# Retention attention followed by two FFN layers on one core: chunk 6 and a decay table loaded behind more weight halves, and VectorE's work of an early step in another order

## The chip, the cores and the metric

The kernel runs on one core of one Trainium2 chip. The metric is the device time of one execution in microseconds. Five engines run side by side, each through its own list of instructions in order: TensorE (PE; its weight loads are shown as PEld), VectorE (DVE), ScalarE (ACT), GpSimd (POOL) and SyncE (SP), which here only issues transfers.

## What is computed

The reference first runs a linear attention with decay ("retention") over 768 positions for 2 batches and 8 heads of 64, and then two feed-forward layers of width 512 to 2048 to 512, the first with Mish, the second with ELU:

```python
for t in range(S):
    state = gamma * state + einsum('bhd,bhe->bhde', k[:, :, t], v[:, :, t])
    y[:, :, t] = scale * einsum('bhd,bhde->bhe', q[:, :, t], state)
x = y.transpose(0, 2, 1, 3).reshape(1536, 512)
h = x @ w_in                      # layer 0
x = (h * tanh(softplus(h))) @ w_out
h = x @ w_in2                     # layer 1
out = where(h > 0, h, exp(min(h, 0)) - 1) @ w_out2
```

## The kernel before

**Retention in chunks.** The positions are cut into 12 chunks of 128 (6 for each batch, taken in turn, numbered 0 to 11). A chunk c has two loads of 512 KB, `qk` and `kv`. GpSimd multiplies its q by a decay table into `qd` (`scale_q`, L202; four of the tables, `tab`, are loaded by `load_tab`) and its k by another into `kd` (`scale_k`, L187). From chunk 4 on, TensorE does a chunk in two parts. `scores64` makes the score products (L304) and the state products (L311, from `kd`); its second half, the function `rest` that it returns, is VectorE's: two mask multiplies into `at` (L319) and one or two state sums (L326). `attend64` then multiplies states by `qd` (L348) and v by `at` (L355); its `rest` is a copy of one part on ScalarE (`t`, L367), two sums on VectorE (`y`, L370), the rounded high part on ScalarE (`xh`, L372) and the low part on VectorE (`xl`, L374). There is one buffer each for `at`, `kd` and `qd`, three for `qk` and `kv`.

**The feed-forward layers.** Every fp32 product is made of three passes with operands split into a high part and a low part. A "tile" n is one 128-wide slice of a layer's 2048 hidden columns against 512 positions. `up(n)` is 12 matmuls (L396): 4 with high weights `w0h`, 4 with low weights `w0l`, 4 with the low part of x. `mish(n)` evaluates Mish twice on ScalarE (`gh`, then `h` itself, L416 and L417) and takes the low part `gl` as their difference on VectorE (L418). `down(n - 3)` is 12 matmuls (L453), three tiles later.

**Weights.** They come as 64-bit words and are unpacked on the chip, in 64 halves k of 512 KB through four staging buffers `st`. For a half: `fetch` issues the load (L109); `dec_fields` extracts fields on ScalarE (L116, L118); `dec_join` puts the bits together on VectorE (L127 for all its halves, then L133), and issues the next `fetch`, which waits for that L133, because it reuses the buffer; `dec_split` rounds to `w0h` or `w1h` on ScalarE (L146) and takes `w0l` or `w1l` as the difference on GpSimd (L147). Half 3 is the first half of weight chunk 3, which `up(3)` reads.

**The order** is written out by hand. After a prologue (chunks 0 to 3 and the first three halves) a loop runs over n = 0, 1, 2, ...; `steps` says which chunk parts belong to a step:

```python
steps = {0: [(scores64, 4, ta)], 3: [(attend64, 6), (scores64, 7)], 4: [(attend64, 7)]}
for n in (1, 2):
    steps[n] = [(attend64, n + 3, tb), (scores64, n + 4, ta)]
```

In a step come: `up(n)` and the matmuls of the chunk parts, `mish(n)`, the `rest` functions with `scale_k` and `scale_q` and `load_chunk` around them (L596 to L605), `dec_split` of the halves joined in the step before, `dec_join` of those started, and `dec_fields` of new ones. All loads go through SP's one queue, in the order of these calls; an issue that has to wait holds back those behind it.

Of the kernel before, what the change touches and what calls it, by code (L numbers as in the profile page):

```python
# [9 lines left out]
F32 = mybir.dt.float32  # L10
# [4 lines left out]
ALU = mybir.AluOpType  # L15
# [8 lines left out]
NCH = B * CPB  # L24
# [11 lines left out]
LAG = 3  # L36
# [7 lines left out]
def retention_then_two_ffn(  # L44
# [7 lines left out]
    nc = tc.nc  # L52
# [49 lines left out]
    def fetch():  # L102
        nonlocal fetched
        if fetched == NHALF:
            return
        n, i = halves[fetched]
        t = stage.tile([P, HC, 2], I32, tag="st", name="st")
        src = w[n, :, i * HC:(i + 1) * HC].bitcast(I32)
        nc.sync.dma_start(out=t.rearrange("p c i -> p (c i)"), in_=src)  # L109
        words[fetched] = t  # L110
        fetched += 1
# [53 lines left out]
    def load_qk(c):  # L165
        t = qk_p.tile([P, 2, NPAIR, P], F32, tag="qk", name="qk")
        nc.sync.dma_start(out=t.rearrange("p a j t -> p (a j t)"), in_=qkv[c, :, :2 * DM])
        return t

    def load_kv(c):  # L170
        t = kv_p.tile([P, 2, H, D], F32, tag="kv", name="kv")
        nc.sync.dma_start(out=t.rearrange("p a h d -> p (a h d)"), in_=qkv[c, :, 2 * DM:])
        return t

    def load_chunk(c):
        raw[c] = (load_qk(c), load_kv(c))
# [28 lines left out]
    def load_tab(i):  # L205
        tabs[i] = qd_p.tile([P, NPAIR, P], F32, tag="tab", name="tab", bufs=2)
        at = N_CT + (i - 2) * N_TQ
        nc.sync.dma_start(
            out=tabs[i].rearrange("p j t -> p (j t)"), in_=consts[:, at:at + N_TQ]
        )  # L210
# [176 lines left out]
    hs, es, gs, accs, acc_ps = {}, {}, {}, {}, {}  # L387
# [24 lines left out]
    def mish(n):  # L412
        h = hs.pop(n)
        gh = gpool.tile([P, TB], F32R, tag="gh", name="gh")
        gl = gpool.tile([P, TB], F32R, tag="gl", name="gl")
        nc.scalar.activation(out=gh, in_=h, func=AF.Mish)  # L416
        nc.scalar.activation(out=h, in_=h, func=AF.Mish)  # L417
        nc.vector.tensor_tensor(out=gl, in0=h, in1=gh.bitcast(F32), op=ALU.subtract)  # L418
        gs[n] = (gh, gl)

    def elu_a(n):
        h = hs[n]
# [62 lines left out]
    with tc.manual_schedule():  # L485
        nc.scalar.preload_act_table_set("mish")
        for s in states:
            nc.vector.memset(s, 0.0)
        qk0 = load_qk(0)
        nc.sync.dma_start(out=ct[:, :N_MASK], in_=consts[:, :N_MASK])  # L490
        raw[0] = (qk0, load_kv(0))
        qk1 = load_qk(1)
        nc.sync.dma_start(out=ct[:, N_MASK:], in_=consts[:, N_MASK:N_CT])
        raw[1] = (qk1, load_kv(1))
        for c, tag in ((2, "xh1"), (3, "xl1")):
            both = xpool.tile([P, KT, TB], F32R, tag=tag, name=tag).bitcast(F32)
            qk, kv = (both[:, 2 * a:2 * a + 2] for a in range(2))
            nc.sync.dma_start(
                out=qk.rearrange("p a n -> p (a n)"), in_=qkv[c, :, :2 * DM]
            )  # L500
            raw[c] = (
                qk.rearrange("p a (j t) -> p a j t", t=P),
                kv.rearrange("p a (h d) -> p a h d", d=D),
            )
        def load_early_kv(c):
            nc.sync.dma_start(
                out=raw[c][1].rearrange("p a h d -> p (a h d)"), in_=qkv[c, :, 2 * DM:]
            )

        fetch()  # L510
        load_early_kv(2)
        load_early_kv(3)
        fetch()
        started = done = 0
        N = len(tiles)

        def room(k, now):
            if k >= NHALF:
                return False
            n, i = halves[k]  # L520
            old = n - GRP - (EXTRA if "w" in late else 0)
            return old < 0 or last_use[old] + LAG * i <= now

        ta, th, tb = ("a0", "a1"), ("h", "h"), ("a2", "a3")
        for i in range(3):
            warm = psa.tile([P, NPAIR, P], F32, tag=f"a{i}", name="warm")
            nc.tensor.matmul(warm, states[0][:, 0], states[0], start=True, stop=True)
        scale_k(0)
        scores(0, ta)()
        scale_k(1)  # L530
        scores(1, th)()
        for c, tags in ((0, tb), (1, th)):
            rests = attend(c, tags[0]), add_state(c, tags[1])
            for rest in rests:
                rest()
        load_chunk(4)
        fetch()
        load_chunk(5)
        load_tab(2)
        fetch()  # L540
        load_chunk(6)
        scale_q(2)
        scale_q(3)
        scores(2, ta)()
        scores(3, th)()
        dec_fields(0)
        dec_join(0)
        scale_k(2)

        lower = mask[half[1]].rearrange("p r j t -> p (r j) t")  # L550
        nc.gpsimd.tensor_copy(lower[:, :, half[0]], lower[:, :, half[1]])
        scale_k(3)
        rests = attend(2, tb[0]), attend(3, tb[1]), add_state(2, "h"), add_state(3, "h")
        rests[0]()
        dec_split(0)
        rests[1]()
        dec_fields(1)
        dec_join(1)
        scale_k(CPT)
        dec_split(1)  # L560
        rests[2]()
        rests[3]()
        dec_fields(2)
        scale_q(CPT)
        dec_join(2)
        done, joined, started, credit = 2, 3, 3, 0.0

        load_tab(3)
        steps = {0: [(scores64, 4, ta)], 3: [(attend64, 6), (scores64, 7)], 4: [(attend64, 7)]}
        for n in (1, 2):  # L570
            steps[n] = [(attend64, n + 3, tb), (scores64, n + 4, ta)]
        for c in range(2 * CPT, NCH):
            n = FIRST + 2 * (c - 2 * CPT)
            steps[n], steps[n + 1] = [(scores64, c)], [(attend64, c)]
        for n in range(N + LAG):
            todo = steps.get(n, [])
            rests = []
            if n < N:
                up(n)
                if todo:  # L580
                    f, *args = todo[0]
                    rests.append(f(*args))
            full = down(n - LAG) if n >= LAG else []
            for f, *args in todo[1:]:
                rests.append(f(*args))
            first_layer = n < N and tiles[n][0] == 0
            if first_layer:
                mish(n)
            elif n < N:
                elu_a(n)  # L590
            if 1 <= n <= N and tiles[n - 1][0] == 1:
                elu_b(n - 1)
            if full and not full[0][1]:
                for e in full:
                    evacuate(*e)
            for (f, c, *_), rest in zip(todo, rests):  # L596
                if f is scores64 and c + 1 < NCH:
                    scale_k(c + 1)
                rest()
                if f is attend64 and c + 3 < NCH:  # L600
                    load_chunk(c + 3)
                if f is attend64 and c + 1 < NCH:
                    scale_q(c + 1)
                    if c % B and (c + 1) // B + 1 < CPB:
                        load_tab((c + 1) // B + 1)  # L605
            for k in range(done, joined):
                dec_split(k)
            done = joined
            if full and full[0][1]:
                for e in full:  # L610
                    evacuate(*e)
            if 1 <= n <= N and tiles[n - 1][0] == 1:
                split(n - 1)
            if any(f is attend64 and c == NCH - 1 for f, c, *_ in todo):
                actx.close()
                late["acc"] = ctx.enter_context(pool("acc12", 1))
                late["m"] = ctx.enter_context(pool("tmp2", 2))
                late["w"] = ctx.enter_context(pool("w2", EXTRA))
            if later:
                later.pop(0)()  # L620
            dec_join(*range(joined, started))
            joined = started
            ahead = range(started, min(started + 2 * GRP, NHALF))
            credit += max([1.0] + [
                (k - started + 1) / max(need[k] - n - 2, 0.5) for k in ahead
            ])
            credit = min(credit, 2.0)
            while credit >= 1 and room(started, n):
                dec_fields(started)
                started += 1  # L630
                credit -= 1


def _consts():
# [54 lines left out]
```

## Time and profile before

| | |
|---|---|
| time, median of 3 runs | 586.96 us (585.64 to 587.08) |
| the profiled execution's own time | 587.08 us |
| its span, from first to last instruction | 585.3 us |
| TensorE busy | 568.0 us (97%) |
| VectorE, ScalarE, GpSimd busy | 320.4, 282.1, 201.6 us |
| mean granted TensorE clock | 0.994 |
| HBM read, over the span | 48.00 MB, 87 GB/s with what is written |

The span lies inside the execution's own time; 1.8 us are outside of it. TensorE's busy share by 5 us stretches is under 90% only in the first 10 us, from 25 to 30, 35 to 45, 55 to 60 and 65 to 70 us; from 70 us on it is 100%. All that a change of order in the early steps can do to the time shows there. A row of the timeline gives start and length in us, engine, line, operation, output and input, the form and a count, and in brackets the idle time of the engine before it with what ended it.

### The profile page before, as it was taken

To read this page: it belongs to the slowest core of one execution; us is meant where nothing else is said; L and a number is where in the kernel's file an instruction comes from. 1 tells how busy PE (TensorE), PEld (TensorE's weight loads), DVE (VectorE), ACT (ScalarE), POOL (GpSimd) and SP (SyncE) were. 2 spreads that over 40 slices of the span, in tenths; PEclk is the share of its full clock that TensorE was granted. 3 is DMA by queue.
4 is the path that set the end of the run, shared out by engine and by line. 5 is a ranking of instruction groups with operands and counts; after the bars stand their busy time and mean duration, and the time that the engine had idled before them with its cause. 6 is when DMAs were issued, how large, how long until landed. Compare 5 with 4: busy or idle time off the path is not lost.

```text
span 585.3 us, 8785 instructions
## 1 busy us (share of the span) xinstructions
PE 568.0 (97%) x3510; PEld 466.5 (80%) x3510; DVE 320.4 (55%) x432; ACT 282.1 (48%) x506; POOL 201.6 (34%) x151
## 2 busy tenths in 40 slices
PE   7967999999999999999999999999999999999997
PEld 5756788888888888888888888888888888888885
DVE  3857755432655553310775996234797774534524
ACT  1555546344654652222665684434875753233331
POOL 2644433301222222110361595221565552222221
PEclk9988999999999999999999999999999999999999
DMA  8968642202242332000233232000333100100101
GB/s 326 394 237 271 199 144 74 74 1 72 77 140 76 106 108 73 0 1 0 97 120 109 72 108 73 1 0 1 109 109 108 37 0 1 72 1 0 73 0 72
DMA packets 15304, 51.70 MB, mean 88 GB/s; under 512 B 1696, under 2 KB 1696, under 8 KB 15264
## 3 DMA queue, kind: packets, MB, share of 16 engines
q1 hardware_dynamic: 15264, 51.15, 25.1%
q8 instruction: 27, 0.44, 0.3%
q14 instruction: 13, 0.11, 0.1%
HBM read 48.00 MB, written 3.15 MB: 87 GB/s over the span
## 4 chain that ended last, share of the span: by engine, by line
PE 88%; DVE 1%; POOL 0%; ACT 0%; issue 0%; POOLq 0%
PE a L453 44%; PE h L396 43%; PE y L348 1%; DVE acc L466 0%; PE y L355 0%; PE sc L304 0%; PE sc L311 0%; POOL w0l L147 0%; DVE y L370 0%; DVE xl L374 0%; ACT t L367 0%; ACT xh L372 0%; POOLq L147 0%
## 5 line engine op out<-in xcount | busy, mean ns | idle before, releaser
L396 PE MATMUL h<-xh,w0h 128*128 128x512 f32 x384 | 103.8, 392 | 2.5 <-ACT w0h L146 2.5
L409 POOL TENSOR_TENSOR gl<-m,gh 128x512 fp32r<-128x512 f32 x48 | 69.6, 1449 | 106.1 <-ACT gh L408 106.1
L396 PE MATMUL h<-xh,w0l 128*128 128x512 f32 x384 | 103.9, 393 | 2.0 <-POOL w0l L147 1.9
L418 DVE TENSOR_TENSOR gl<-h,gh 128x512 fp32r<-128x512 f32 x48 | 33.2, 691 | 130.8 <-ACT h L417 126.9
L396 PE MATMUL h<-xl,w0h 128*128 128x512 f32 x384 | 103.0, 390 | 0.0
L426 ACT ACTIVATE e<-c 128x512 f32<-128x512 f32 x48 | 30.4, 633 | 123.3 <-DVE c L425 123.3
L147 POOL TENSOR_TENSOR w0l<-f,w0h 128x512 fp32r<-128x512 f32 x32 | 42.7, 1337 | 135.1 <-ACT w0h L146 126.0
L425 DVE TENSOR_SCALAR c<-h 128x512 f32<-128x512 f32 x48 | 33.1, 690 | 101.8 <-PE h L396 101.7
L416 ACT ACTIVATE gh<-h 128x512 fp32r<-128x512 f32 x48 | 28.6, 597 | 121.3 <-PE h L396 121.3
L396 PEld LDWEIGHTS h<-xh,w0l 128*128 128x128 f32 x384 | 72.2, 189 | 18.5 <-POOL w0l L147 3.7
L396 PEld LDWEIGHTS h<-xh,w0h 128*128 128x128 f32 x384 | 71.8, 188 | 17.9 <-ACT w0h L146 3.0
L396 PEld LDWEIGHTS h<-xl,w0h 128*128 128x128 f32 x384 | 72.5, 189 | 15.3
L453 PE MATMUL a<-gh,w1h 128*128 128x512 f32 x192 | 75.8, 395 | 0.0
L453 PE MATMUL a<-gl,w1h 128*128 128x512 f32 x192 | 74.8, 390 | 0.0
L453 PE MATMUL a<-gh,w1l 128*128 128x512 f32 x192 | 74.8, 390 | 0.0
L453 PE MATMUL a<-w1h,gh 128*128 128x512 f32 x192 | 74.7, 389 | 0.0
L453 PE MATMUL a<-w1l,gh 128*128 128x512 f32 x192 | 74.7, 389 | 0.0
L453 PE MATMUL a<-w1h,gl 128*128 128x512 f32 x192 | 74.7, 389 | 0.0
L133 DVE SCALAR_TENSOR_TENSOR f<-f,st 128x512 int32<-128x512 int32 x64 | 69.7, 1098 | 3.8
L127 DVE SCALAR_TENSOR_TENSOR st<-st 128x512 int32<-128x512 int32 x64 | 71.3, 1123 | 0.6 <-ACT st L118 0.6
L147 POOL TENSOR_TENSOR w1l<-f,w1h 128x512 fp32r<-128x512 f32 x32 | 45.7, 1429 | 61.5 <-ACT w1h L146 48.4
L116 ACT ACTIVATE f<-st 128x512 f32<-128x512 f32 x64 | 42.8, 668 | 10.1 <-DMA st<-w 6.2
(80 smaller groups left out, 691.8 us busy)
## 6 DMA issues: line engine op xcount, KB each, us to landing
st<-w SPq DMA_DIRECT2D x64, 512.0 KB, 3.6
qk<-qkv SPq DMA_DIRECT2D x10, 512.0 KB, 7.6
kv<-qkv SPq DMA_DIRECT2D x10, 512.0 KB, 8.2
out<-acc SPq DMA_DIRECT2D x12, 256.0 KB, 2.1
xh<-qkv SPq DMA_DIRECT2D x2, 512.0 KB, 9.4
xl<-qkv SPq DMA_DIRECT2D x2, 512.0 KB, 10.0
tab<-consts SPq DMA_DIRECT2D x4, 256.0 KB, 8.6
ct<-consts SPq DMA_DIRECT2D x1, 512.0 KB, 5.7
```

Of the source, the lines that this page charges most:

```text
L116: nc.scalar.activation(out=f, in_=t[:, :, 1].bitcast(F32), func=AF.Copy, scale=2.0 ** -112)
L127: nc.vector.scalar_tensor_tensor(out=t[:, :, 1], in0=t[:, :, 1], scalar=-(2 ** 31), in1=t[:, :, 0], op0=ALU.bitwise_and, op1=ALU.bitwise_or,)
L133: nc.vector.scalar_tensor_tensor(out=f, in0=f, scalar=3, in1=t[:, :, 1], op0=ALU.logical_shift_left, op1=ALU.bitwise_or,)
L147: nc.gpsimd.tensor_tensor(out=lo, in0=f, in1=hi.bitcast(F32), op=ALU.subtract)
L348: nc.tensor.matmul(y[r][sl, far, j], state[m][sl, j], qd[sl, j, half[m]], start=j == 0 and far == 1, stop=far == 1, skip_group_check=True,)
L396: nc.tensor.matmul(h, u[:, k * P:(k + 1) * P], v[:, k], start=i == 0, stop=i == len(passes) - 1)
L409: nc.gpsimd.tensor_tensor(out=gl, in0=g, in1=gh.bitcast(F32), op=ALU.subtract)
L416: nc.scalar.activation(out=gh, in_=h, func=AF.Mish)
L418: nc.vector.tensor_tensor(out=gl, in0=h, in1=gh.bitcast(F32), op=ALU.subtract)
L425: nc.vector.tensor_scalar(out=c, in0=h, scalar1=0.0, scalar2=None, op0=ALU.min)
L426: nc.scalar.activation(out=e, in_=c, func=AF.Exp)
L453: nc.tensor.matmul(a, l, r, start=first and i == 0, stop=last and i == 2)
```

## The change

Two things are moved; no operation is added or taken away.

Loads: chunk 6 and table 3, which were issued in the prologue, are issued at the end of step 0; chunk c + 3 is issued at the end of a step that has `attend64` of c, not in the middle, and so behind the `fetch` calls of the step's `dec_join`.

VectorE's order: `mish` returns its subtraction (the low part) to be placed later. In steps 1 and 2 the two `rest` functions are taken in reversed order, scores first; and the low part comes behind them. In step 3 it stays ahead of them; in the later steps of layer 0 it comes behind.

```diff
@@ mish @@
-        nc.vector.tensor_tensor(out=gl, in0=h, in1=gh.bitcast(F32), op=ALU.subtract)
-        gs[n] = (gh, gl)
+        def rest():
+            nc.vector.tensor_tensor(out=gl, in0=h, in1=gh.bitcast(F32), op=ALU.subtract)
+            gs[n] = (gh, gl)
+        return rest
@@ prologue @@
         load_chunk(5)
         load_tab(2)
         fetch()
-        load_chunk(6)
         scale_q(2)
...
-        load_tab(3)
         steps = {0: [(scores64, 4, ta)], 3: [(attend64, 6), (scores64, 7)], 4: [(attend64, 7)]}
@@ the loop over n @@
             if first_layer:
-                mish(n)
+                low = mish(n)
...
-            for (f, c, *_), rest in zip(todo, rests):
+            pairs = list(zip(todo, rests))
+            if n < LAG:
+                pairs.reverse()
+            elif first_layer and len(todo) > 1:
+                low()
+                low = None
+            for (f, c, *_), rest in pairs:
                 if f is scores64 and c + 1 < NCH:
                     scale_k(c + 1)
                 rest()
-                if f is attend64 and c + 3 < NCH:
-                    load_chunk(c + 3)
                 if f is attend64 and c + 1 < NCH:
                     scale_q(c + 1)
                     if c % B and (c + 1) // B + 1 < CPB:
                         load_tab((c + 1) // B + 1)
+            if first_layer and low:
+                low()
...
+            if n == 0:
+                load_chunk(6)
+                load_tab(3)
+            for f, c, *_ in todo:
+                if f is attend64 and c + 3 < NCH:
+                    load_chunk(c + 3)
```

Where that puts the instructions is shown at three places, before and after. First SP's queue from the load of half 3 on, before: `st` are weight halves (218 is half 3, 259, 323 and 342 are 4 to 6, 528 and 531 are 7 and 8), `qk_220` and `kv_222` are chunk 6, `qk_512` and `kv_514` chunk 7, `tab_344` is table 3.

```order
L109 DMA st_218<-w 128x1024
L167 DMA qk_220<-qkv 128x1024
L172 DMA kv_222<-qkv 128x1024
L109 DMA st_259<-w 128x1024
L109 DMA st_323<-w 128x1024
L109 DMA st_342<-w 128x1024
L208 DMA tab_344<-consts 128x512
L167 DMA qk_512<-qkv 128x1024
L172 DMA kv_514<-qkv 128x1024
L109 DMA st_528<-w 128x1024
L109 DMA st_531<-w 128x1024
```

And SP's queue after the change from the same load on; here `qk_409` and `kv_411` are chunk 6, `st_524` and `st_527` halves 7 and 8, `qk_535` and `kv_537` chunk 7.

```order
L109 DMA st_218<-w 128x1024
L109 DMA st_255<-w 128x1024
L109 DMA st_319<-w 128x1024
L109 DMA st_338<-w 128x1024
L167 DMA qk_409<-qkv 128x1024
L172 DMA kv_411<-qkv 128x1024
L208 DMA tab_413<-consts 128x512
L109 DMA st_524<-w 128x1024
L109 DMA st_527<-w 128x1024
L167 DMA qk_535<-qkv 128x1024
L172 DMA kv_537<-qkv 128x1024
```

Chunk 6 has moved behind halves 4, 5 and 6, and chunk 7 behind halves 7 and 8, whose issues wait for the joins of halves 3 and 4.

Second, GpSimd from the `kd` of chunk 5 (step 0) to the first low weights of step 2, before; `kv_222` and `kv_514` are chunks 6 and 7, `qk_212` and `qk_220` chunks 5 and 6, and `w0l_650` is half 3.

```order
L187 TENSOR_TENSOR kd_398<-kv_214,ct_94 128x512
L147 TENSOR_TENSOR w0l_406<-f_335,w0h_405 128x512
L202 TENSOR_TENSOR qd_516<-qk_212,tab_216 128x512
L187 TENSOR_TENSOR kd_518<-kv_222,ct_94 128x512
L202 TENSOR_TENSOR qd_638<-qk_220,tab_344 128x512
L187 TENSOR_TENSOR kd_642<-kv_514,ct_94 128x512
L147 TENSOR_TENSOR w0l_650<-f_409,w0h_649 128x512
L147 TENSOR_TENSOR w1l_654<-f_412,w1h_653 128x512
```

And GpSimd after the change at the same place, where `kv_411` and `kv_537` are chunks 6 and 7 and `w0l_646` is half 3.

```order
L187 TENSOR_TENSOR kd_391<-kv_214,ct_94 128x512
L147 TENSOR_TENSOR w0l_400<-f_331,w0h_399 128x512
L187 TENSOR_TENSOR kd_500<-kv_411,ct_94 128x512
L202 TENSOR_TENSOR qd_518<-qk_212,tab_216 128x512
L187 TENSOR_TENSOR kd_624<-kv_537,ct_94 128x512
L202 TENSOR_TENSOR qd_640<-qk_409,tab_413 128x512
L147 TENSOR_TENSOR w0l_646<-f_403,w0h_645 128x512
L147 TENSOR_TENSOR w1l_650<-f_406,w1h_649 128x512
```

In each of steps 1 and 2 `kd` and `qd` have changed places: the one for the chunk after next comes first.

Third, VectorE at the end of step 0 and in step 1, before: `at_400` and `state0_95` belong to the scores of chunk 4, `y`, `xl1` to `attend64` of chunk 4.

```order
L418 TENSOR_TENSOR gl_394<-h_346,gh_393 128x512
L319 TENSOR_TENSOR at_400<-sc_359,ct_94 128x256
L319 TENSOR_TENSOR at_400<-sc_360,ct_94 128x256
L326 TENSOR_TENSOR state0_95<-sc_359,compact0_97 128x256
L326 TENSOR_TENSOR state0_95<-sc_360,state0_95 128x256
L418 TENSOR_TENSOR gl_497<-h_415,gh_496 128x512
L370 TENSOR_TENSOR y_429<-y_429,t_503 64x256
L370 TENSOR_TENSOR y_428<-y_428,t_503 64x256
L374 TENSOR_TENSOR xl1_502<-y_428,xh1_501 128x4x64
L374 TENSOR_TENSOR xl1_502<-y_429,xh1_501 128x4x64
```

And VectorE after the change from the same place on; `at_502` and `state1_96` belong to the scores of chunk 5.

```order
L319 TENSOR_TENSOR at_393<-sc_353,ct_94 128x256
L319 TENSOR_TENSOR at_393<-sc_354,ct_94 128x256
L326 TENSOR_TENSOR state0_95<-sc_353,compact0_97 128x256
L326 TENSOR_TENSOR state0_95<-sc_354,state0_95 128x256
L420 TENSOR_TENSOR gl_388<-h_340,gh_387 128x512
L319 TENSOR_TENSOR at_502<-sc_462,ct_94 128x256
L319 TENSOR_TENSOR at_502<-sc_463,ct_94 128x256
L326 TENSOR_TENSOR state1_96<-sc_462,compact1_98 128x256
L326 TENSOR_TENSOR state1_96<-sc_463,state1_96 128x256
L370 TENSOR_TENSOR y_429<-y_429,t_509 64x256
```

The masks and states of chunk 5 now stand ahead of the sums `y` of chunk 4 and of the low part of Mish, where they stood behind both.

## Rows read from the trace of the kernel before

**Rows 1.** Timeline of TensorE, steps 1 to 4.

```profile
31.21 0.66 PE L311 MATMUL sc<-kv,kd 64*64 64x64 f32 x31
...
33.76 1.08 PE L396 MATMUL h<-xl,w0h 128*128 128x512 f32 x4
38.89 0.24 PE L348 MATMUL y<-qd,state 64*64 64x64 f32 x1 [4.05 <-DVE state L326]
...
45.43 1.65 PE L396 MATMUL h<-xh,w0h 128*128 128x512 f32 x4 [2.45 <-ACT w0h L146]
46.88 2.00 PE L396 MATMUL h<-xh,w0l 128*128 128x512 f32 x4
48.67 1.42 PE L396 MATMUL h<-xl,w0h 128*128 128x512 f32 x4
...
58.19 1.20 PE L396 MATMUL h<-xh,w0l 128*128 128x512 f32 x4 [1.39 <-POOL w0l L147]
```

**Rows 2.** Busy time by engine in one stretch; granted clock, DMA share, GB/s.

```profile
45.00:50.00 5.00, 4.57 (x12) 3.15 (x12) 4.96 (x10) 3.04 (x6) 2.54 (x2) 0.66 0.97 259
```

**Rows 3.** Timeline of VectorE, step 1 and the start of step 2.

```profile
34.91 0.69 DVE L418 TENSOR_TENSOR gl<-h,gh 128x512 fp32r<-128x512 f32 x1 [5.28 <-ACT h L417]
35.62 0.88 DVE L370 TENSOR_TENSOR y<-y,t 64x256 f32<-64x256 f32 x2
...
37.67 0.74 DVE L319 TENSOR_TENSOR at<-sc,ct 128x256 f32<-128x256 f32 x2
...
39.12 1.28 DVE L127 SCALAR_TENSOR_TENSOR st<-st 128x512 int32<-128x512 int32 x2
40.32 2.37 DVE L133 SCALAR_TENSOR_TENSOR f<-f,st 128x512 int32<-128x512 int32 x2
```

**Rows 4.** Timeline of ScalarE, steps 0 to 2.

```profile
28.79 0.67 ACT L116 ACTIVATE f<-st 128x512 f32<-128x512 f32 x1 [0.67 <-DMA st<-w]
...
32.69 0.67 ACT L116 ACTIVATE f<-st 128x512 f32<-128x512 f32 x1 [2.66 <-DMA st<-w]
...
34.80 0.76 ACT L367 COPY t<-y 64x256 f32<-64x256 f32 x2
```

**Rows 5.** Timeline of SP's queue; the time is that of the issue.

```profile
22.57 5.28 SPq L109 DMA_DIRECT2D st<-w  x3
...
31.01 0.33 SPq L172 DMA_DIRECT2D kv<-qkv  x1
41.07 2.03 SPq L109 DMA_DIRECT2D st<-w  x2
...
43.66 0.38 SPq L172 DMA_DIRECT2D kv<-qkv  x1
...
61.05 0.93 SPq L109 DMA_DIRECT2D st<-w  x2
...
62.55 0.38 SPq L172 DMA_DIRECT2D kv<-qkv  x1
```

**Rows 6.** Timeline of GpSimd, steps 2 and 3.

```profile
40.82 1.31 POOL L202 TENSOR_TENSOR qd<-qk,tab 128x512 f32<-128x512 f32 x1 [7.52 <-PE y L348]
43.16 1.04 POOL L187 TENSOR_TENSOR kd<-kv,ct 128x512 f32<-128x512 f32 x1 [1.03 <-DVE f L133]
45.46 1.29 POOL L147 TENSOR_TENSOR w0l<-f,w0h 128x512 fp32r<-128x512 f32 x1 [1.25 <-ACT w0h L146]
...
55.87 1.05 POOL L187 TENSOR_TENSOR kd<-kv,ct 128x512 f32<-128x512 f32 x1 [3.25 <-PE sc L311]
56.87 1.26 POOL L147 TENSOR_TENSOR w0l<-f,w0h 128x512 fp32r<-128x512 f32 x1
```

**Rows 7.** Issues at 41.07, 43.66, 62.55: KB each, us to landing.

```profile
st<-w SPq DMA_DIRECT2D x1, 512.0 KB, 3.5
kv<-qkv SPq DMA_DIRECT2D x1, 512.0 KB, 8.5
kv<-qkv SPq DMA_DIRECT2D x1, 512.0 KB, 8.3
```

## The prediction, before the changed kernel was run

> **What bounds the kernel now.** I read the busy shares by stretch first: from 70 us on TensorE is never idle, so only what delays it before that can change the time. Then the timeline of TensorE over the early steps, where the brackets name what it waited for [rows 1]. It shows three places. After `up(2)` ends at 34.84 (33.76 + 1.08) TensorE idles 4.05 us until 38.89, where `attend64` of chunk 5 gets its state from VectorE. After the scores of chunk 6 it idles 2.45 us until 45.43, where `up(3)` gets the high weights of half 3. And it idles 1.39 us at 58.19, in `up(4)`, for low weights from GpSimd. The idle time also costs clock: four matmuls of one pass, 1.08 us at 33.76, take 2.00 us at 46.88 [rows 1], and the granted clock of 45 to 50 us is 0.66, a mixture of the lower level (1.2 GHz) and the full one (2.4) [rows 2].
>
> Next I followed the wait at 38.89 back. VectorE did masks and states of chunk 5 only at 37.67, behind `gl` (34.91), which had waited 5.28 us for ScalarE, and behind the sums `y` (35.62) [rows 3]. ScalarE was late because its `dec_fields` of half 4, in line ahead of Mish, waited for its load until 32.69 [rows 4]. Yet the products of chunk 5 were done at 31.87 (31.21 + 0.66) [rows 1]. So both edits aim at a true wait of 4.05 us. What matters is what comes late in its place.
>
> **The change, part by part.** I give times on the clock of the old trace.
>
> *Half 4 earlier.* In the old queue halves 3 and 4 have the two loads of chunk 6 between them; they land at 28.79 and 32.69, three loads in 3.90 us, so 1.30 each [rows 4]. The queue is full here: half 6 is issued by 27.85 (22.57 + 5.28) [rows 5], before the ones ahead of it are in. So half 4 lands at 30.1, half 5 at 31.4, half 6 at 32.7, `qk` of chunk 6 at 34.0 and its `kv` at 35.3. ScalarE's Mish of step 1 and the copies `t` come 2.6 us earlier: `t` starts at 32.2 instead of 34.80 [rows 4] and ends at 33.0.
>
> *Chunk 6 later.* GpSimd's list now has `kd` of chunk 6 ahead of `qd` of chunk 5. `kd` starts when `kv` lands, 35.3; it takes 1.0 and `qd` 1.3 [rows 6], so `qd` of chunk 5 is there at 37.65 and `attend64` can start at 37.7, 1.2 us before the old 38.89. Of the 4.05 us only that much is won; the rest of the wait changes its owner, from VectorE to GpSimd and behind it the load.
>
> *VectorE in the new order.* The gain of at most 0.7 us (one `gl`) for `attend64` of chunk 4 puts the products of chunk 5 at 31.5. Masks and states take 1.45 (37.67 to 39.12), `y` and `xl` with the high part between them 2.05 (35.62 to 37.67), `gl` 0.71 [rows 3]: states done at 33.0, `xl` at 35.0, `gl` at 35.7. Then come the joins of halves 3 and 4. The pair of L127 takes 1.2. The pair of L133, the same form, took 2.37 [rows 3] with one GpSimd multiply of 1.31 beside it at 40.82 [rows 6], about 1.1 more than a pair alone. Alone the joins would end at 38.2; two such operations (`kd` and `qd` at 35.3 to 37.65) run beside them, which makes 40.4 at most. `kd` begins before the joins, so I take 39.7, and 39.0 for the first of the two L133.
>
> *Chunk 7 much later: the main term.* Before, its `kv` was issued at 31.01 [rows 5], and its `kd` ran at 43.16 [rows 6] without having to wait for it. Now chunk 7 stands behind halves 7 and 8, whose issues wait for those two L133: half 7 goes out at 39.0, half 8 at 39.7, `qk` and `kv` of chunk 7 by 40.6. How soon `kv` lands the old trace shows from both sides. One half alone, issued at 41.07 into an idle queue, lands after 3.5 us [rows 5, 7]; with three more loads at 1.30, the pace of the full queue, that is 7.4 us. But the like groups of two halves, `qk` and `kv` took longer: `kv` issued at 62.55 landed 8.3 later, 9.8 after the first half at 61.05; `kv` issued at 43.66 landed 8.5 later, 11.1 after the half at 41.07, there with the second half itself late [rows 5, 7]. While that group moved, the stretch of 45 to 50 us shows the engines of the DMA busy for 0.97 of the time at 259 GB/s [rows 2]. The group at 61.05 is the nearest in form. Here GpSimd stands idle, so I take a little less, 9.0: `kv` of chunk 7 lands at 48.0. The bounds are 45.0 (37.6 + 7.4) and 50.6 (39.5 + 11.1).
>
> The Trainium skill (DMA: Bandwidth & Descriptors, section "Anatomy of one DMA — SWDGE (gpsimd) path") fits a transfer, on the path that GpSimd issues, by about 2.0 us and its bytes at 436 GB/s; by it a half takes 3.2 us where this trace has 3.5, and by that estimate four loads in a row take 6.8 us and `kv` lands at 45.8, which would take 2.2 us off the sum below. The rows of the three groups are slower than that, so the sum doesn't use it.
>
> *Who is queued behind that load.* GpSimd's list of step 2 is `kd` of chunk 7, `qd` of chunk 6, low weights of half 3, low weights of half 4; before, `qd` of chunk 6 came first and both its loads had long landed. The lengths are 1.0, 1.3 and 1.29 [rows 6], so the low weights of half 3 are there at 48.0 + 3.6 = 51.6. The second pass of `up(3)` reads them; it began at 46.88 [rows 1]. The first pass, freed by ScalarE's high weights at about 44 to 45.5, does not help, since TensorE takes the passes in order. So TensorE is 4.7 us behind the old trace at this place.
>
> *Clock.* TensorE idles some 6 us before that pass; the old trace shows the lower level after idle times of 4.05 and 2.45 us. Passes two and three took 3.2 us from 46.88 to 50.1, the last part at the full level; wholly at the lower one they take 2 x 1.8 (46.88 to 48.67) = 3.6 [rows 1]. I add 0.4, and 0.1 for the first products of `attend64` of chunk 6 behind it. At the full level it would be 1.2 less than the old 3.2.
>
> *What follows.* The wait of 1.39 us at 58.19 hangs on `kd` of chunk 8, which waited for TensorE's own products (3.25 us, 55.87) and held the low weights at 56.87 [rows 6]; it moves along with TensorE and gives nothing back. Half 7 and chunk 8 have some 4 us of room there. In the steps of layer 0 after that, the low part stands behind 1.5 to 2 us of chunk work, but `down` reads it three steps later: nothing. From 70 us on TensorE has no idle time in which a delay could be made good.
>
> **Sum.** 4.7 + 0.5 = +5.2 us. The profiled execution took 587.08 us, 0.12 above the median, so 592.3 by its own time and 592.2 against the median.
>
> **The rivals.**
>
> *Fast transfers.* The loads of chunk 7 move at the pace of the full queue, since fewer engines work beside them. `kv` then lands at 45.0 to 46.5, the second pass starts 1.8 to 3.2 us late, and a full clock could give back up to 1.2: +0.6 to +3.2, or 587.6 to 590.2 us. For it: 1.30 a load in the early trace. Against it: no group after 40 us shows it. Chance 0.15, of which 0.06 lies within 0.3%.
>
> *Faster.* GpSimd isn't held, and only the wait that was aimed at is gone. The point that decides is the landing of `kv` of chunk 7: at 43.2 or earlier (46.88 - 3.6) the second pass isn't late. Then `attend64` of chunk 5 and `up(3)` start 1.2 us earlier, and with a clock that doesn't fall up to 2.8 more is won in 39 to 50 us: -1.2 to -4.0, 583 to 585.8 us. Against it: the half ahead would have to go out at 35.8, when VectorE still does `gl`. It would also come if GpSimd could take the ready work first; the list says it can't, and `kd` of chunk 8 held the low weights in the same way [rows 6]. The Trainium skill (TensorE: Matmul & The Clock Gate, section "Architectural detail: the array is 16× 32×32, not 1× 128×128", on queue depths) calls GpSimd's queue strictly first in, first out, which agrees. Chance 0.07, of which 0.01 within 0.3%.
>
> *Worse.* As forecast, but the group of loads is as slow as the one at 41.07: +7 to +8, 594 to 595. Chance 0.08.
>
> **The numbers.** The forecast, +2.6 to +7.0, has 0.70. About 0.3% (1.8 us) is what a measurement can tell here. Slower: 0.70 + 0.08 + 0.09 = 0.87; same 0.06 + 0.01 = 0.07; faster 0.06. The range of 589.6 to 594.0 leaves out the rivals' ends, under 2 in 10.
>
> **What the profile after would show.** `kd` of chunk 6 starting at about 35.3 and `attend64` of chunk 5 at 37.7, both released by GpSimd and a load; joins ending near 39.7; GpSimd idle until `kv` of chunk 7 lands near 48; the second pass of `up(3)` waiting some 6 us for `w0l` of L147, and starting near 51.6 at the lower clock. The prediction is wrong if `kd` of chunk 7 starts by 43, or if later waits of TensorE (58.19) shrink by what the early one grew.

## The result, and the profile after

The changed kernel is slower: 593.94 us median (593.46 to 594.12, 4 runs) against 586.30 us of the kernel before in the same comparison (585.47 to 587.08, 4 runs); ratio 1.0124, 95% interval 1.0105 to 1.0142. The span of the profiled execution is 592.2 us, 6.9 more than before.

| | before | after |
|---|---|---|
| span, us | 585.3 | 592.2 |
| TensorE busy, us | 568.0 | 570.3 |
| mean granted TensorE clock | 0.994 | 0.986 |
| VectorE, ScalarE, GpSimd busy, us | 320.4, 282.1, 201.6 | 321.2, 282.5, 201.8 |

The work is the same: 3510 matmuls in both traces. TensorE's 2.3 us more of busy time go with the lower mean clock, and the other 4.6 us are idle time. TensorE's timeline of the changed kernel answers to [rows 1]:

```profile
39.09 0.37 PE L348 MATMUL y<-qd,state 64*64 64x64 f32 x1 [4.67 <-POOL qd L202]
...
47.37 1.97 PE L396 MATMUL h<-xh,w0h 128*128 128x512 f32 x4 [3.75 <-ACT w0h L146]
53.41 2.08 PE L396 MATMUL h<-xh,w0l 128*128 128x512 f32 x4 [4.06 <-POOL w0l L147]
55.28 1.91 PE L396 MATMUL h<-xl,w0h 128*128 128x512 f32 x4
...
65.50 1.20 PE L396 MATMUL h<-xh,w0l 128*128 128x512 f32 x4 [1.33 <-POOL w0l L147]
```

The wait ahead of `attend64` of chunk 5 is no shorter (4.67 us for 4.05), but its releaser is now GpSimd's `qd`. A new wait of 4.06 us stands ahead of the second pass of `up(3)`, which starts at 53.41 for 46.88. The wait in `up(4)` is the old one, 7.31 us later.

GpSimd's timeline of the changed kernel shows why; it answers to [rows 6]:

```profile
36.27 1.09 POOL L187 TENSOR_TENSOR kd<-kv,ct 128x512 f32<-128x512 f32 x1 [5.16 <-DMA kv<-qkv]
37.33 1.71 POOL L202 TENSOR_TENSOR qd<-qk,tab 128x512 f32<-128x512 f32 x1
48.89 1.13 POOL L187 TENSOR_TENSOR kd<-kv,ct 128x512 f32<-128x512 f32 x1 [9.85 <-DMA kv<-qkv]
49.98 1.71 POOL L202 TENSOR_TENSOR qd<-qk,tab 128x512 f32<-128x512 f32 x1
51.65 1.71 POOL L147 TENSOR_TENSOR w0l<-f,w0h 128x512 fp32r<-128x512 f32 x1
```

Twice its next instruction is a `kd` whose load hasn't landed: 5.16 us for chunk 6 and 9.85 us for chunk 7. The `qd` and the low weights that TensorE waits for stand behind it. The loads, from SP's queue (answers to [rows 5]):

```profile
28.08 0.37 SPq L172 DMA_DIRECT2D kv<-qkv  x1
...
39.65 1.84 SPq L109 DMA_DIRECT2D st<-w  x2
...
42.06 0.38 SPq L172 DMA_DIRECT2D kv<-qkv  x1
```

and their times to landing, in windows around the issues at 28.08 and 42.06 (answers to [rows 7]):

```profile
kv<-qkv SPq DMA_DIRECT2D x1, 512.0 KB, 8.0
kv<-qkv SPq DMA_DIRECT2D x1, 512.0 KB, 6.7
```

`kv` of chunk 7 goes out at 42.06, behind two halves that waited for VectorE's joins, and lands at 48.8 (42.06 + 6.7), 9.1 us after the first of those halves. `kv` of chunk 6 lands at 36.1.

### The profile page after: what moved, and what is told of

Same layout as the page of the kernel before. It is cut to its first block, busy times and chain, and to the rows that moved or that the text cites. A ratio compares the mean times of both kernels' runs of the same rounds, so it can differ in the third digit from the quotient of the medians.

```text
span 592.2 us, 8781 instructions
## 1 busy us (share of the span) xinstructions
PE 570.3 (96%) x3510; PEld 467.8 (79%) x3510; DVE 321.2 (54%) x432; ACT 282.5 (48%) x506; POOL 201.8 (34%) x151
## 4 chain that ended last, share of the span: by engine, by line
PE 87%; DVE 1%; POOL 0%; ACT 0%; issue 0%; POOLq 0%
PE a L457 43%; PE h L396 42%; PE y L348 1%; DVE acc L470 0%; PE y L355 0%; PE sc L304 0%; PE sc L311 0%; POOL w0l L147 0%; DVE y L370 0%; DVE xl L374 0%; ACT t L367 0%; ACT xh L372 0%; POOLq L147 0%
## 5 line engine op out<-in xcount | busy, mean ns | idle before, releaser
L147 POOL TENSOR_TENSOR w0l<-f,w0h 128x512 fp32r<-128x512 f32 x32 | 42.4, 1326 | 132.6 <-ACT w0h L146 125.6
L127 DVE SCALAR_TENSOR_TENSOR st<-st 128x512 int32<-128x512 int32 x64 | 73.3, 1154 | 0.8 <-ACT st L118 0.8
L147 POOL TENSOR_TENSOR w1l<-f,w1h 128x512 fp32r<-128x512 f32 x32 | 45.3, 1416 | 61.6 <-ACT w1h L146 50.5
```

What stands on the lines that cost most here:

```text
L127: nc.vector.scalar_tensor_tensor(out=t[:, :, 1], in0=t[:, :, 1], scalar=-(2 ** 31), in1=t[:, :, 0], op0=ALU.bitwise_and, op1=ALU.bitwise_or,)
L147: nc.gpsimd.tensor_tensor(out=lo, in0=f, in1=hi.bitcast(F32), op=ALU.subtract)
```

## The experiments

Theory A is that of the prediction: GpSimd takes its list in order, and the loads of chunks 6 and 7, now late, hold what stands behind their `kd`. Rival B: VectorE's new order itself costs. Rival C: the late chunk 6 is what costs. Rival D: the slow group of loads delays the work wherever `kd` stands. In the comparison of the first four kernels the kernel before took 586.37 us (19 runs), in that of the last four 586.53 us (17 runs).

**Order alone.** Loads in their old places, the rest as changed:

```diff
         fetch()
+        load_chunk(6)
         scale_q(2)
...
+        load_tab(3)
...
                 rest()
+                if f is attend64 and c + 3 < NCH:
+                    load_chunk(c + 3)
...
-            if n == 0:
-                load_chunk(6)
-                load_tab(3)
-            for f, c, *_ in todo:
-                if f is attend64 and c + 3 < NCH:
-                    load_chunk(c + 3)
```

> All loads stand in their old places; VectorE's new order and GpSimd's kd ahead of qd stay. Theory A (GpSimd's list is held by the kv loads of chunks 6 and 7, which the new load places make late): GpSimd's kd of chunks 6 and 7 run near 32 and 43 us, up(3) starts its second pass within 1 us of the old 46.88, and the time is 585.5 to 587.5 us, no change from before; attend64 of chunk 5 starts near 37.8, since xl of chunk 4 (its PSUM) still comes behind the late half 4. Rival B (VectorE's new order itself costs: sums y behind masks that wait for TensorE, joins and high weights later): most of the 7 us stays, 591 to 594 us.

Measured: 587.03 us (10 runs), ratio 1.0007 (0.9994 to 1.0020): no change. B falls: the order alone doesn't cost the 7 us. TensorE and then GpSimd in this run:

```profile
37.55 0.30 PE L348 MATMUL y<-qd,state 64*64 64x64 f32 x2 [3.19 <-DVE xl L374]
...
45.20 1.89 PE L396 MATMUL h<-xh,w0h 128*128 128x512 f32 x4 [3.56 <-ACT w0h L146]
```

```profile
41.78 1.04 POOL L187 TENSOR_TENSOR kd<-kv,ct 128x512 f32<-128x512 f32 x1 [7.86 <-PE sc L311]
```

GpSimd's wait is for TensorE's own products, not for a load. The order brings `attend64` of chunk 5 forward by 1.3 us, to where `xl` of chunk 4 frees its PSUM tiles, and `up(3)` gives it back: its high weights stand on ScalarE behind `xh` of chunk 5.

**Loads alone.** Loads as changed, VectorE and GpSimd in the old order:

```diff
+            if first_layer:
+                low()
+                low = None
             pairs = list(zip(todo, rests))
-            if n < LAG:
-                pairs.reverse()
-            elif first_layer and len(todo) > 1:
-                low()
-                low = None
```

> Only the loads are in their new places; VectorE and GpSimd work in the old order. Theory A: kd of chunk 7 still stands ahead of the low weights of half 3 and waits for its kv until 48 to 49 us; with qd of chunk 6 ahead of it, the second pass of up(3) starts near 51.5: +4.5 to +5.5, 591 to 592 us. Rival B: 586 to 588 us, since the order is the old one. Rival C (the late chunk 6 with its 4.67 us wait is what costs, not chunk 7): 586 to 588 us, since qd of chunk 5 no longer stands behind chunk 6.

Measured: 592.63 us (4 runs), ratio 1.0097 (1.0072 to 1.0122). B's and C's figures for this run (586 to 588 us) are out. A's wait is there, and the time is 0.6 us above A's range of 591 to 592. GpSimd, then TensorE:

```profile
48.65 1.04 POOL L187 TENSOR_TENSOR kd<-kv,ct 128x512 f32<-128x512 f32 x1 [6.59 <-DMA kv<-qkv]
49.65 1.26 POOL L147 TENSOR_TENSOR w0l<-f,w0h 128x512 fp32r<-128x512 f32 x1
```

```profile
50.97 2.07 PE L396 MATMUL h<-xh,w0l 128*128 128x512 f32 x4 [6.39 <-POOL w0l L147]
```

`kd` of chunk 7 has its load at 48.65 here too, and TensorE's wait for the low weights behind it is 6.39 us.

**Chunk 7 early.** As changed, but chunk c + 3 in the middle of the step again; chunk 6 stays late:

```diff
                 rest()
+                if f is attend64 and c + 3 < NCH:
+                    load_chunk(c + 3)
...
-            for f, c, *_ in todo:
-                if f is attend64 and c + 3 < NCH:
-                    load_chunk(c + 3)
```

> As the changed kernel, but chunk c + 3 is loaded in the middle of a step again, ahead of the fetches of that step; chunk 6 and table 3 stay at the end of step 0. Theory A: kv of chunk 7 lands near 38.5, GpSimd waits only for chunk 6 (36.3 us); attend64 of chunk 5 stays at 39.1, up(3) at about 47 for its high weights, its second pass follows at 48.5 to 49.5: +2 us, 587.5 to 589.5. Rival B and rival C: 592 to 594, since both the order and the late chunk 6 are still there.

Measured: 588.73 us (10 runs, a wide 586.61 to 591.91), ratio 1.0038 (1.0017 to 1.0058), within A's range. The profiled execution took 590.99 us, 2.3 above the median, and its TensorE is 2.0 us later than the changed kernel's already at `attend64` of chunk 4 (30.93 for 28.93 us); so I read its waits, not its start times. TensorE has no wait for low weights left in `up(3)`; the one for chunk 6 stays:

```profile
41.61 0.36 PE L348 MATMUL y<-qd,state 64*64 64x64 f32 x1 [5.18 <-POOL qd L202]
```

So of the 1.24%, some two thirds by the medians come with the late loads of chunk 7 and the chunks behind it (1.0124 against 1.0038; the intervals leave about half to nine tenths), and the rest with the late chunk 6 in the new order.

**kd last in steps 1 and 2.** As changed, all loads late, but `kd` put behind GpSimd's other work of the step:

```diff
-                if f is scores64 and c + 1 < NCH:
+                if f is scores64 and c + 1 < NCH and n not in (1, 2):
                     scale_k(c + 1)
...
             done = joined
+            if n in (1, 2):
+                scale_k(n + 5)
```

> As the changed kernel, all loads in their new, late places, but in steps 1 and 2 GpSimd's kd is put behind qd and the weights' low parts of the step, so that ready work is not held. Theory A: qd of chunk 5 is there by 33 us, attend64 of chunk 5 starts near 35.3, up(3) near 43, its second pass near 45, 2 us ahead of the kernel before; kd of chunk 7 near 50 still comes in time for step 3: 583.5 to 585.5 us. Rival B: 591 to 594 us. Rival D (the slow group of loads itself delays the work, not the place in GpSimd's list): 590 us or more, with TensorE waiting for the scores of chunk 7 instead.

Measured: 591.02 us (4 runs), ratio 1.0075 (1.0047 to 1.0102). The time is 5.5 us above A's range; D's figure is met, and B's (591 to 594) too, but B is out by the run with the order alone. GpSimd in this run:

```profile
43.98 1.28 POOL L147 TENSOR_TENSOR w0l<-f,w0h 128x512 fp32r<-128x512 f32 x1 [5.39 <-ACT w0h L146]
...
48.93 1.04 POOL L187 TENSOR_TENSOR kd<-kv,ct 128x512 f32<-128x512 f32 x1 [1.99 <-DMA kv<-qkv]
...
58.19 1.32 POOL L187 TENSOR_TENSOR kd<-kv,ct 128x512 f32<-128x512 f32 x1 [6.64 <-DMA kv<-qkv]
59.48 1.25 POOL L147 TENSOR_TENSOR w0l<-f,w0h 128x512 fp32r<-128x512 f32 x1
```

The low weights of half 3 run at 43.98, for 51.65 in the changed kernel: step 2 is as expected. But TensorE, now early, meets the same wait one step on: `kd` of chunk 8, in step 3, waits for its `kv` until 58.19, with the low weights of half 5 behind it. In the changed kernel that load had landed (near 61.6) when its `kd` came up at 63.18, since everything else was late. D's mechanism, TensorE waiting for the products of chunk 7, isn't in the trace: its largest waits are for ScalarE's high weights in `up(3)` (5.98 us) and for the low weights in `up(4)` (5.03 us). The next run decides.

**kd last in step 3 too.** `(1, 2, 3)` for `(1, 2)` in both places.

> As the kernel with kd last in steps 1 and 2, and now in step 3 too, where kd of chunk 8 held the low weights of half 5 until 58 us. All loads stay in their new places. Theory A (late kv loads cost only because GpSimd's list holds other work behind them): the second pass of up(4) starts near 55.6 without a wait, TensorE is some 2.6 us ahead of the kernel before: 583 to 584.5 us. Rival D (the slow loads delay the work wherever they stand): TensorE waits for products of chunk 7 or 8 instead, 589 us or more.

Measured: 584.14 us (12 runs), ratio 0.9964 (0.9951 to 0.9976): within A's range, and faster than the kernel before, with every load in its late place. GpSimd, then TensorE:

```profile
53.51 1.27 POOL L147 TENSOR_TENSOR w0l<-f,w0h 128x512 fp32r<-128x512 f32 x1 [2.03 <-ACT w0h L146]
...
57.94 1.52 POOL L187 TENSOR_TENSOR kd<-kv,ct 128x512 f32<-128x512 f32 x1 [1.89 <-DMA kv<-qkv]
```

```profile
43.67 2.07 PE L396 MATMUL h<-xh,w0h 128*128 128x512 f32 x4 [5.64 <-ACT w0h L146]
```

`kd` of chunk 8 gets its load about as late as in the last run, at 57.94 for 58.19, and nothing that TensorE needs soon stands behind it. D falls: with the loads still late, none of TensorE's waits between 30 and 70 us is for work behind a late load. Whether these three moves would gain more with the loads in their old places, no run tests. Against the changed kernel only the place of three GpSimd instructions differs, and it is worth 1.6% of the time of the kernel before (1.0124 to 0.9964).

**Weights split first.** What was left in front of `up(3)` is that wait of 5.64 us for ScalarE, whose high weights stood behind `xh` of chunk 5. To the last kernel, with chunk c + 3 loaded in the middle of the step again:

```diff
+            if n in (2, 3):
+                for k in range(done, joined):
+                    dec_split(k)
+                done = joined
             pairs = list(zip(todo, rests))
```

> As the one with kd last in three steps, with two more moves: chunk c + 3 is loaded in the middle of a step again, and in steps 2 and 3 the weights joined in the step before are rounded and split ahead of the chunks' work, so that ScalarE's high weights of half 3 don't stand behind xh of chunk 5. By theory A: up(3) starts near 40.5 in place of 43.95, at the full clock, with no wait behind it until 70 us: 579.5 to 581.5 us. By a rival in which GpSimd's or VectorE's own work is the limit of these steps: no better than the one with kd last in three steps.

Measured: 580.99 us (4 runs), ratio 0.9903 (0.9890 to 0.9917), within the range expected and faster than both kernels; the rival's "no better" is out. Two things differ from the last kernel, and no run takes them apart. `up(3)` starts at 39.90 and its second pass at 41.28, and the mean granted clock is 1.000. TensorE still waits a little, where I had expected no wait behind the start of `up(3)`; its largest waits between 30 and 55 us:

```profile
39.90 1.20 PE L396 MATMUL h<-xh,w0h 128*128 128x512 f32 x4 [1.18 <-ACT w0h L146]
...
51.22 1.20 PE L396 MATMUL h<-xh,w0h 128*128 128x512 f32 x4 [1.61 <-DVE xl L374]
```

**Old loads.** The same with chunk 6 and table 3 back in the prologue.

> As the one with weights split first, with chunk 6 and table 3 back in the prologue, so that all loads are in the places of the kernel before. It tells what the earlier halves 4 to 6 are worth once nothing is held behind late chunks. Mine: half 4 lands at 32.7, attend64 of chunk 5 starts at 37.6, up(3) near 41.7: 581.5 to 583 us, 1.5 to 2 us slower than the one with weights split first. If the load places are worth nothing: the same time as that one.

Measured: 582.05 us (5 runs), ratio 0.9919 (0.9906 to 0.9932). The median is 1.1 us above that of the last kernel, on the side that I expected, but the intervals overlap: what the earlier halves are worth stays unsettled by time. The trace shows the mechanism, `attend64` of chunk 5 at 37.59 for 35.94. (The profiled execution is the slowest of the five, 583.51 us.)

**Before, split first.** The kernel before, with its own loads and VectorE's old order, and only the two moves (kd last in steps 1 to 3, weights split first in steps 2 and 3).

> The kernel before, with its own load places and VectorE's old order, and only kd last in steps 1 to 3 and the weights split first in steps 2 and 3. It tells what the new order of VectorE is worth beside the two moves. Mine: attend64 of chunk 5 at 38.9 as before, up(3) at 43.0 without the wait of 2.45, no wait of 1.39 in up(4): 582.5 to 584 us. If VectorE's new order brings nothing: as the one with old loads and the new order.

Measured: 582.86 us (5 runs), ratio 0.9941 (0.9929 to 0.9953). It is within the range expected, with `up(3)` at 42.96 for my 43.0. Most of the gain of the best kernel thus comes from the two moves. What VectorE's new order adds with the old loads, 0.8 us by the medians, isn't settled, since the intervals overlap a little. New order and late chunk 6 together are worth 1.9 us (582.86 to 580.99, intervals apart): the change's own aim pays once nothing is held behind the late loads.

## Why the prediction was right

*The number.* The forecast was +5.2 us, to 592.2. Measured are +7.6 by the medians, and 6.9 between the two profiled executions (587.08 and 593.94). The median lies 0.06 us inside the upper end of the range, and that is in part luck: in this comparison the kernel before took 586.30 us, 0.66 less than the median that I added to, and the change of 7.6 is more than the +7.0 at which my range ended. It is the size of the rival *Worse* (+7 to +8), whose condition, a group of loads that takes 11.1 us, did not come: the group took 9.1. So the mechanism was right, and its size was too small.

*The main term.* Chunk 7 behind the joins, its `kd` ahead of the low weights of half 3: shown from both sides. Moving the load back removes the wait for the low weights (1.0038), and moving `kd` behind them removes it with the load still late (the run with kd last in steps 1 and 2).

*Its size was too small.* The forecast for the second pass of `up(3)` was 51.6; it started at 53.41. Half of the 1.8 us is the load: `kd` of chunk 7 starts at 48.89, where I had 48.0, mostly because half 7 goes out at 39.65 for my 39.0. The other half lies in GpSimd's three operations, 4.5 us from 48.89 to the pass for my 3.6: `qd` and the low weights took 1.71 each, where I took 1.3. VectorE's timeline of the changed kernel has the joins of halves 3 and 4, then those of halves 5 and 6, just at that place:

```profile
35.78 2.13 DVE L127 SCALAR_TENSOR_TENSOR st<-st 128x512 int32<-128x512 int32 x2
37.84 2.35 DVE L133 SCALAR_TENSOR_TENSOR f<-f,st 128x512 int32<-128x512 int32 x2
...
49.03 3.20 DVE L133 SCALAR_TENSOR_TENSOR f<-f,st 128x512 int32<-128x512 int32 x2
```

I had counted what GpSimd does to the joins [rows 3], and not what the joins do to GpSimd. A join beside it isn't enough for that: the `qd` of 1.31 us at 40.82 that I took my figure from also had joins beside it [rows 3, 6]. It began 0.2 us before one join ended and 0.1 us before the next began. In the changed kernel the two operations of 1.71 us, at 49.98 and 51.65, each began with 0.6 us of a join still to run. Over the ten traces, the 103 operations of L147 and L202 that began with 0.5 us or more of a join to run took 1.66 to 1.76 us; the 531 that began with no join running took 1.26 to 1.31, among them 254 that had a join beside them later. The joins of halves 3 and 4 end at 40.2, where I had 39.7.

*Chunk 6.* The step was right, its size off, and it is no term of the sum: `kv` landed at 36.1 for 35.3, `qd` took 1.71, and `attend64` of chunk 5 started at 39.09 for 37.7, so that nothing of the 4.05 us was won.

*Clock.* The second and third pass took 3.8 us (53.41 to 57.19), for 3.2 before and a forecast of 3.6, and `attend64` of chunk 6 some 0.2 more.

*What follows.* The shift was 7.31 us at 65.50 and 6.9 at the end of the span. As forecast, the wait in `up(4)` moved along and gave nothing back. The 0.4 us came back in `up(5)`, where the wait for low weights was 0.55 us and is now 0.18; I had not looked at that one. Behind it TensorE has no idle time until its last matmul, as forecast.

*The rivals.* Fast transfers did not come: 9.1 us from the first half to the landing of `kv`, where I took 9.0 and the pace of the full queue gives 7.4. The Trainium skill's fit for a transfer (DMA: Bandwidth & Descriptors, "Anatomy of one DMA — SWDGE (gpsimd) path"), which came to 6.8 us by estimate, is further off than the rows; these loads are issued by SP, not on that path. The faster rival's condition, that GpSimd isn't held, is met in the run with kd last in three steps, and it is then faster by 0.36%: 584.14 us, in that rival's range.

## What to carry to other kernels

When a load moves, list what stands behind the first instruction that reads it, on that engine; a wait moved from one engine to another in front of older, ready work can cost more than it saved. A lateness that was cured in two steps showed up in the third, where the same order stood, so a cure is judged after all of them. An instruction that prepares data for a later step, and whose load may be late, was better placed behind the work of its own step (1.0124 against 0.9964 here).

## What was not expected of the hardware

The clock was granted late. One-microsecond stretches of the changed kernel (busy time of PE, PEld, DVE, ACT, POOL, then granted clock, DMA share, GB/s):

```profile
38.00:39.00 1.00, 0.00 (x0) 0.00 (x0) 1.00 (x1) 0.00 (x0) 1.00 (x1) 0.50 0.00 0
...
42.00:43.00 1.00, 1.00 (x50) 1.00 (x46) 0.00 (x0) 0.73 (x2) 0.00 (x0) 0.50 0.97 299
...
45.00:46.00 1.00, 0.00 (x0) 0.00 (x0) 0.95 (x3) 0.00 (x0) 0.00 (x0) 1.00 0.94 377
...
56.00:57.00 1.00, 1.00 (x3) 0.37 (x2) 0.00 (x0) 0.00 (x0) 0.00 (x0) 0.50 0.80 258
```

TensorE was granted the full level (2.4 GHz) at 45 us, when it idled, and the lower one (1.2 GHz) at 42 and at 56 us, when it was busy throughout.

The group of loads after 40 us moves more slowly than the 1.30 us a load of the prologue, though GpSimd stands idle: 9.1 us to the last landing, where that pace gives 7.4. The stretch from 42 to 43 us has 299 GB/s with GpSimd and VectorE idle and the DMA engines busy for 0.97 of it; three microseconds later, with VectorE at work, it is 377. My thought that an idle GpSimd makes the loads faster is not borne out by these stretches; what slows some of them stays open.

When a join on VectorE and an operation on GpSimd meet, the one that starts second is the longer. A join that began with GpSimd idle took 0.68 to 0.70 us in all ten traces, one that began beside a GpSimd operation of the program's lines up to 1.82; the other direction is the 1.66 to 1.76 for 1.26 to 1.31 us above. The added time shows as busy time of the engine, not as a wait.
